# Attention with decay and a switch mixture of experts: from pairs of heads over 512 tokens to 64x64 TensorE tiles over all heads

## Chip, cores and metric

One Trainium2 chip, one core of it. The metric is the device time of one launch in microseconds, and the median of three runs of the kernel before is 514.04 us (512.87 to 514.76). The profile is one execution of its own.

## What is computed

q, k and v have 8 batches, 8 heads, 576 tokens and 64 channels each, in f32. Scores are weighted by a decay per head, without softmax; the 4608 rows of 512 channels then go each to one of 8 experts.

```python
scores = scale * np.matmul(q, k.transpose(0, 1, 3, 2))
gamma = 1.0 - 2.0 ** (-5.0 - np.arange(H, dtype=np.float32))
Dmat = np.where(rel >= 0, gamma[:, None, None] ** rel[None, :, :], 0.0)
ret = scores * Dmat[None, :, :, :]
attn_out = np.matmul(ret, v)
x = attn_out.transpose(0, 2, 1, 3).reshape(B * S, H * D)
logits = x @ w_gate
expert_idx = np.argmax(logits, axis=1)
# gate_w: the chosen expert's softmax probability
out[mask] = gate_w[mask, None] * (np.maximum(xe @ w1[e], 0.0) @ w2[e])
```

## The kernel before

The decay is put into q and k ahead of the products (kg, qg: powers of gamma by position), so a score needs a causal mask alone. What lies further back than the current chunk of 128 tokens comes from a state, the sum of k^T v over the earlier chunks.

**Attention.** The loop runs over units (b, p): for each of 8 batches four units with a pair of heads and 512 tokens in four chunks, and a fifth with the last 64 tokens of all heads. Five functions make a unit. `stage_T` (lines 221 to 258) scales kk and qq on GpSimd, transposes both on TensorE into psq and psk, and copies them to qT (VectorE) and kT (ScalarE). `stage_S` (260 to 274) sums the states of all four chunks with products of 128x64 by up to 256 columns into pss; ScalarE copies them to sall. `stage_SC` (276 to 300) makes scores of 128x128 per head in psa and psb, one head on the upper half of the rows and one on the lower; VectorE multiplies them by the mask tri into sa and sb. `stage_AV` (302 to 326) adds scores times v and state times q in psx, copied to xT. `stage_XR` (330 to 359) turns xT back into rows with a product by iw, the identity with the gate's weights beside it: so rows and logits come at once; ScalarE writes xr in bf16, VectorE adds up lg, and SyncE's queue writes x_rows to DRAM.

TensorE's order is the program's order, fixed by `pin`: SC of a unit, XR of the one ahead, T and S of the next, AV of this one. The other engines' lists are made by a scheduler, and each engine works its list off in order. q, k and v of batch b+1 are asked for at the head of batch b, into two sets of buffers.

**Routing.** The tokens are routed in two halves (g = 0 and 1). `softmax_top1` and `ranks` give each token its expert and its place there; `place` makes one-hot rows rh by place and pay by expert, and a product of them, pspl, gives the list of tokens by slot. Each expert has 256 slots for the first half (ph 0, two blocks) and 384 for all that is left (ph 1, three blocks). The first half is routed amid batches 4 and 5; the second has to wait for the last batch.

**Experts.** `load_w` (line 200) brings a piece of 128x1024 f32 weights into one of four staging buffers and casts it to bf16. A piece of w1 is written in another order of its columns than it is read (line 211). The pieces of experts 0 and 1 come in the attention, one in every second unit, with GpSimd as the named caster; later ones in turn on ScalarE, VectorE and GpSimd (line 594). Three experts' weights have room. Per expert and phase, `gather` fetches rows by an indirect transfer, `trans` transposes them (line 553) into xt, `mm1` (557) multiplies by w1 and takes Relu on ScalarE into ht, `mm2` (573) multiplies by w2, VectorE scales by the gate's weight into ys, and GpSimd issues an indirect transfer to out.

```python
198:    casts = [nc.gpsimd.tensor_copy, nc.scalar.copy, nc.vector.tensor_copy]
211:            casts[eng](out=w1b[:, c, :, :, :].rearrange("p j s m -> p j m s"),
212:                       in_=st[:, :].rearrange("p (j m s) -> p j m s", m=P, s=2))
285:                    mm(ps[:, c, :], kT[r, c * P:(c + 1) * P], qT[r, c * P:(c + 1) * P], True, True)
312:                    mm(psx[j * DH:(j + 1) * DH, c, :], vt[:, c, 2 * p + j, :], d["sc"][j][:, c, :], c == 0, False)
314:                mm(psx[:, c, :], sl[:, p, c - 1, :], qT[:, c * P:(c + 1) * P], False, c == NCH - 1)
```

## Time and profile before

| | |
|---|---|
| median of three runs | 514.04 us |
| the profiled execution | 518.02 us, its span 516.2 us |
| TensorE products, busy | 407.9 us (79%), 3714 records |
| VectorE, ScalarE, GpSimd, busy | 197.2, 186.9, 277.0 us |
| mean granted clock of TensorE | 0.903 of 2.4 GHz |
| moved by DMA | 82.0 MB, 159 GB/s in the mean |

Busy time is an average over stages with different limits, so it is read by stretch. An f32 product has two records on TensorE, a transpose or a bf16 product one. A record's time runs until its result is written; how fast TensorE works is read from the starts of records that follow each other. In a row of a group stands: line, engine, operation, output<-inputs, shapes, count | busy us, mean ns of one | idle us ahead of them and what ended it.

### The profile page before, as it was taken

The numbers are of one execution on the slowest core, as the hardware profiler recorded it, in microseconds if no ns is written. First come the engines' busy times: TensorE is split into PE (matmuls) and PEld (weight loads), VectorE is DVE, ScalarE is ACT, GpSimd is POOL, SyncE is SP. The second block draws the span as 40 slices with busy tenths as digits, with TensorE's granted clock in tenths as the row PEclk, the third lists the DMA queues.
The fourth block names the chain that finished last, engine by engine and source line by source line (L and its number), as shares of the span: only waits on it lengthen the run. The fifth ranks groups of instructions, "written<-read, shape, count | busy, mean of one in ns | idle before, by whom it ended". The sixth has DMA issues, their size and how long they took to land. (4 is left out here: it accounts for less than half of the span.)

```text
span 516.2 us, 9296 instructions
## 1 busy us (share of the span) xinstructions
PE 407.9 (79%) x3714; PEld 303.6 (59%) x3714; DVE 197.2 (38%) x398; ACT 186.9 (36%) x300; POOL 277.0 (54%) x237
## 2 busy tenths in 40 slices
PE   0999999999997999899857777769196590999930
PEld 0888888888876888688735433436044150555610
DVE  4333333333668333533397232554033260233210
ACT  1343334344332344943310163429334160423400
POOL 9433546943475778731034767746646576452320
PEclk9999999999998999899995968869789596899985
DMA  9978989694975979640100326456562653321120
GB/s 207 241 146 205 222 192 255 165 252 134 247 179 127 229 229 279 235 178 1 48 22 28 102 83 253 155 193 249 194 217 89 238 176 139 111 103 74 57 86 12
DMA packets 107509, 81.98 MB, mean 159 GB/s; under 512 B 82879, under 2 KB 95679, under 8 KB 107457
## 3 DMA queue, kind: packets, MB, share of 16 engines
q1 hardware_dynamic: 102336, 66.61, 47.2%
q0 software_dynamic: 5120, 14.69, 8.0%
q8 instruction: 31, 0.51, 0.4%
q14 instruction: 22, 0.17, 0.1%
HBM read 67.13 MB, written 15.20 MB: 159 GB/s over the span
## 5 line engine op out<-in xcount | busy, mean ns | idle before, releaser
L59 PE MATMUL pm<-xt,w1b 128*128 128x256 bf16 (+1 forms) x512 | 79.7, 315 | 31.2 <-ACT ht L570 28.3
L584 POOL DMA_INDIRECT out_dram<-ys,tids x40 | 41.3, 1031 | 113.9 <-DVE ohb L448 29.2
L59 PEld LDWEIGHTS <-w1b 128*128 128x128 bf16 x512 | 52.1, 102 | 57.4 <-issue 35.9
L570 ACT ACTIVATE ht<-pm 128x384 bf16<-128x384 f32 (+1 forms) x96 | 50.0, 535 | 93.3 <-PE pm L59 91.4
L211 POOL CAST w1b<-wst 128x1024 bf16<-128x1024 f32 x16 | 80.0, 5066 | 6.9 <-PE psb L59 2.7
L59 PE MATMUL py<-w2b,ht 128*128 128x512 bf16 x320 | 79.4, 406 | 2.0 <-ACT ht L570 2.0
L231 POOL TENSOR_TENSOR qq<-qt,qg 128x512 f32<-128x512 f32 x32 | 34.8, 1092 | 52.2 <-PE psq L237 37.9
L488 POOL DMA_INDIRECT xg<-x_rows,tidg x40 | 50.3, 1257 | 17.9 <-DVE gat L476 8.4
L289 DVE TENSOR_TENSOR sa<-psa,tri 128x512 f32<-128x512 f32 x32 | 22.4, 700 | 97.8 <-PE psb L59 96.9
L59 PEld LDWEIGHTS <-ht 128*128 128x128 bf16 x320 | 32.4, 104 | 42.2 <-issue 8.0
L59 PE MATMUL psr<-iw,xT 128*128 128x136 f32 (+1 forms) x320 | 48.3, 295 | 4.3 <-ACT xT L316 3.0
L583 DVE TENSOR_SCALAR ys<-py,gat 128x512 f32<-128x512 f32 x40 | 29.8, 753 | 50.4 <-PE py L59 41.9
L59 PE MATMUL psa<-qT,kT 64*128 64x128 f32 (+1 forms) x320 | 43.4, 277 | 3.6 <-DVE qT L242 3.6
L59 PEld LDWEIGHTS psr<-iw,xT 128*128 128x128 f32 (+1 forms) x320 | 39.6, 181 | 9.5 <-ACT xT L316 5.1
L59 PE MATMUL pss<-vt,kk 128*64 128x128 f32 (+3 forms) x512 | 44.0, 317 | 0.0
L59 PE MATMUL psb<-qT,kT 64*128 64x128 f32 (+1 forms) x320 | 43.5, 277 | 0.0
L211 ACT CAST w1b<-wst 128x1024 bf16<-128x1024 f32 x8 | 39.2, 4962 | 8.2 <-DMA wst<-in_moe_w_dram 7.4
L59 PEld LDWEIGHTS psa<-qT,kT 64*128 64x128 f32 (+1 forms) x320 | 36.1, 181 | 8.0 <-issue 3.7
L227 POOL TENSOR_TENSOR kk<-kt,kg 128x512 f32<-128x512 f32 x32 | 33.8, 1056 | 12.8 <-PE pss L59 11.8
L211 DVE CAST w1b<-wst 128x1024 bf16<-128x1024 f32 x8 | 25.9, 3233 | 38.0 <-PE pm L59 25.3
L59 PEld LDWEIGHTS pss<-vt,kk 128*64 128x64 f32 x512 | 33.0, 142 | 12.2 <-issue 6.4
L59 PE MATMUL psx<-qT,sall 128*128 128x128 f32 (+1 forms) x256 | 38.8, 289 | 0.0
(124 smaller groups left out, 615.1 us busy)
## 6 DMA issues: line engine op xcount, KB each, us to landing
wst<-in_moe_w_dram SPq DMA_DIRECT2D x64, 512.0 KB, 4.9
kt<-in_k_dram SPq DMA_DIRECT2D x28, 256.0 KB, 5.5
qt<-in_q_dram SPq DMA_DIRECT2D x7, 1024.0 KB, 7.8
vt<-in_v_dram SPq DMA_DIRECT2D x28, 256.0 KB, 5.1
x_rows<-xr SPq DMA_DIRECT2D x8, 512.0 KB, 3.9
kt<-in_k_dram SPq DMA_DIRECT2D x8, 128.0 KB, 3.8
qt<-in_q_dram SPq DMA_DIRECT2D x4, 256.0 KB, 4.1
vt<-in_v_dram SPq DMA_DIRECT2D x8, 128.0 KB, 3.8
```

The costliest lines, as they stand in the source:

```text
L59: return pin(nc.tensor.matmul(out=out, lhsT=lhsT, rhs=rhs, start=start, stop=stop, skip_group_check=True))
L211: casts[eng](out=w1b[:, c, :, :, :].rearrange("p j s m -> p j m s"), in_=st[:, :].rearrange("p (j m s) -> p j m s", m=P, s=2))
L227: nc.gpsimd.tensor_tensor(out=kk[:, :, :].rearrange("p c (h d) -> p c h d", d=DH), in0=kt[:, :, h0:h0 + 2, :], in1=kg[:, 0:NCH, h0:h0 + 2] ...
L231: nc.gpsimd.tensor_tensor(out=qq[:, :, :].rearrange("p s (h d) -> p h s d", d=DH), in0=qt[:, h0:h0 + 2, :, :], in1=qg[:, 0:NCH, h0:h0 + 2] ...
L289: nc.vector.tensor_tensor(out=sa[:, :, :], in0=psa[:, :, :], in1=m, op=ALU.mult)
L488: nc.gpsimd.indirect_dma_start(out=xg[:, :], out_offset=None, in_=x_rows[0:nr, :], in_offset=bass.IndirectOffsetOnAxis(ap=slots[ph][1][:, ...
L570: nc.scalar.activation(out=ht[:, f0:f0 + per, :], in_=pm[:, :, :], func=AF.Relu)
L583: nc.vector.tensor_scalar(out=ys[:, :], in0=py[:, :], scalar1=gat[:, i:i + 1], scalar2=None, op0=ALU.mult)
L584: nc.gpsimd.indirect_dma_start(out=out[:, :], out_offset=bass.IndirectOffsetOnAxis(ap=tids[:, i:i + 1], axis=0), in_=ys[:, :], in_offset=N ...
```

## The change

The attention goes over blocks (b, c): 128 tokens (c = 0 to 3) of all heads, and the last 64. Scores, the state and the output work in chunks of 64 tokens, all in products of 64x64. S and SC and the first half of AV name four quarters of the array in turn (rows by the half of the operands, columns by the half of the output); the second half of AV, state times q, names the upper left and the lower right one. What the two row halves make goes to two banks: pss and psx have two banks, which VectorE and ScalarE add up (so2, so, se; xo, xT). pss and psx are one tile each for the whole attention. `stage_R` makes rows with transposes, and the gate's logits come once a batch (`stage_L1`, `stage_L2`) with 32 columns of weights per quarter. q of the next batch is transposed in the blocks of this one (`stage_TQ`). TensorE's order per block is S, SC, R of the block ahead, TK of the next, L1, AV, TQ, L2.

w1 and w2 keep their plain layout, so the cast reads and writes straight. The early pieces name ScalarE as caster and come one per block in the last 16 blocks; later ones VectorE, ScalarE, VectorE in turn, GpSimd never. Staging has 3 buffers for 4, gathered rows 6 for 8. `place` is cut in `prep` (all on VectorE), `rows_hot` and the product; the first half's prep for phase 1 moves into the attention.

```diff
-    stpool = ctx.enter_context(tc.tile_pool(name="wstage", bufs=4))
+    stpool = ctx.enter_context(tc.tile_pool(name="wstage", bufs=3))
-    gp = ctx.enter_context(tc.tile_pool(name="gath", bufs=8))
+    gp = ctx.enter_context(tc.tile_pool(name="gath", bufs=6))
...
+    psx = ps1.tile([P, 2, 512], F32, name="psx")
+    nc.vector.memset(psx[:, :, :], 0.0)
+    pss = ps1.tile([P, 2, 512], F32, name="pss")
...
-    casts = [nc.gpsimd.tensor_copy, nc.scalar.copy, nc.vector.tensor_copy]
+    casts = [nc.scalar.copy, nc.vector.tensor_copy, nc.gpsimd.tensor_copy]
...
-            casts[eng](out=w1b[:, c, :, :, :].rearrange("p j s m -> p j m s"),
-                       in_=st[:, :].rearrange("p (j m s) -> p j m s", m=P, s=2))
+            casts[eng](out=w1b[:, c, :], in_=st[:, :])
...
+    def stage_S(b, c):
...
+        for p in range(NP):
+            for par in range(2):
+                r = slice(par * DH, (par + 1) * DH)
+                for j in range(2):
+                    h = 2 * p + j
+                    mm(pss[j * DH:(j + 1) * DH, par, p * DH:(p + 1) * DH], kk[r, h, :], vt[r, c, h, :],
+                       c == 0 and p == 0, c == NCH - 1)
...
+            nc.vector.tensor_tensor(out=fl, in0=e_, in1=sts[(b, c, "oo")][:, :, :].rearrange("p a d -> p (a d)"),
+                                    op=ALU.add)
+        so2 = wkp.tile([P, NP, DH], F32, tag="so2")
+        nc.scalar.copy(out=so2[:, :, :].rearrange("p a d -> p (a d)"), in_=o_)
+        se = wkp.tile([P, NP, DH], F32, tag="se")
+        nc.vector.tensor_tensor(out=se[:, :, :].rearrange("p a d -> p (a d)"), in0=e_,
+                                in1=so2[:, :, :].rearrange("p a d -> p (a d)"), op=ALU.add)
...
+    def stage_SC(b, c):
...
+                    for par in range(2):
+                        t0 = c * P + par * DH
+                        mm(ps[par * DH:(par + 1) * DH, j, p * DH:(p + 1) * DH], kT[r, p, par * DH:(par + 1) * DH],
+                           qT[r, p, t0:t0 + DH], True, True)
...
+        nc.vector.tensor_tensor(
+            out=sc[:, :, 0:n, :], in0=ps[:, :, 0:n * DH].rearrange("p j (a i) -> p j a i", i=DH),
+            in1=tri[:, :].unsqueeze(1).unsqueeze(1).to_broadcast([P, 2, n, DH]), op=ALU.mult)
+
+    def stage_AV(b, c):
...
+                    for j in range(2):
+                        mm(x[j * DH:(j + 1) * DH, par, p, par, :], vt[r, c, 2 * p + j, :], sc[r, j, p, :],
+                           p == 0, False)
+            for p in range(NP):
+                for par in range(2):
+                    for j in range(2):
+                        r = slice(j * DH, (j + 1) * DH)
+                        t0 = c * P + par * DH
+                        mm(x[r, j, p, par, :], (se, so)[par][r, p, :], qT[r, p, t0:t0 + DH], False, p == NP - 1)
...
+        xo = wk1.tile([P, n * P], F32, tag="xo", name="xo")
+        nc.scalar.copy(out=xo[:, :], in_=psx[:, 1, 0:n * P])
...
+        nc.vector.tensor_tensor(out=dst, in0=psx[:, 0, 0:n * P], in1=xo[:, :], op=ALU.add)
...
-        w_at.setdefault(len(units) - 2 * len(early) + 2 * n_, []).append(x_)
+        w_at.setdefault(len(blocks) - len(early) + n_, []).append(x_)
...
+        stage_S(b, c)
+        stage_SC(b, c)
         if i > 0:
-            stage_XR(units[i - 1])
+            stage_R(*blocks[i - 1])
...
+            stage_TK(*blocks[i + 1])
+        if c == 0 and b > 0:
+            stage_L1(b - 1)
+        stage_AV(b, c)
+        if c < NP and b + 1 < B:
+            stage_TQ(b + 1, c)
...
+        if (b, c) == (B // 2 + 2, 0):
+            prep(1, 0, rt)
...
-            load_w(e, pt, (1, 2, 0)[nq[0] % 3])
+            load_w(e, pt, (1, 0, 1)[nq[0] % 3])
...
+            rows_hot(1, 0, rtm2)
+            prep(1, 1, rtm2)
+            rows_hot(1, 1, rtm2)
```

VectorE in the attention, before, one unit with a pair of heads (sa and sb are masked scores, qT the copy of q transposed, lg the logits):

```order
L289 TENSOR_TENSOR sa<-psa,tri 128x512
L290 TENSOR_TENSOR sb<-psb,tri 128x512
L242 COPY qT<-psq 128x512
L350 TENSOR_TENSOR lg<-psr,lg 128x32
L289 TENSOR_TENSOR sa<-psa,tri 128x512
L290 TENSOR_TENSOR sb<-psb,tri 128x512
```

VectorE, the change, two blocks of a batch (in names the list shows so2 as so with a number):

```order
L270 TENSOR_TENSOR so<-pss,so_733 128x256
L275 TENSOR_TENSOR se<-pss,so_864 128x256
L305 TENSOR_TENSOR sc<-pssc,tri 128x512
L354 TENSOR_TENSOR xT<-psx,xo 128x512
L270 TENSOR_TENSOR so<-pss,so_864 128x256
L275 TENSOR_TENSOR se<-pss,so_965 128x256
L305 TENSOR_TENSOR sc<-pssc,tri 128x512
```

The copy of q went to ScalarE, and the sums of the two banks, for the state ahead of the mask and for the output behind it, came to VectorE.

ScalarE, the change, at the start of batch 5 (w2b and w1b are casts of early weights):

```order
L247 COPY kT<-psk 128x512
L346 COPY xo<-psx 128x512
L234 COPY qT<-psq 128x512
L213 CAST w2b<-wst 128x1024 x2
L209 CAST w1b<-wst 128x1024
L273 COPY so_2971<-pss 128x256
L368 CAST xr<-psr 128x512
L247 COPY kT<-psk 128x512
L209 CAST w1b<-wst 128x1024 x2
L346 COPY xo<-psx 128x512
```

Before, these pieces' casts stood in GpSimd's list; here five of them stand among the copies of one block and the next.

GpSimd with the experts, before (xg is a gather, out_dram a scatter):

```order
L584 DMA out_dram<-ys,tids_2041 4608x512 x2
L211 CAST w1b<-wst 128x4x128x2
L488 DMA xg<-x_rows,tidg_3212 128x512 x2
L584 DMA out_dram<-ys,tids_3211 4608x512 x2
L216 CAST w2b<-wst 128x1024
L584 DMA out_dram<-ys,tids_3211 4608x512
```

GpSimd with the experts, the change:

```order
L536 DMA xg<-x_rows,tidg_2946 128x512
L536 DMA xg<-x_rows,tidg_4631 128x512
L643 DMA out_dram<-ys,tids_4630 4608x512 x3
L536 DMA xg<-x_rows,tidg_4631 128x512 x2
L536 DMA xg<-x_rows,tidg_2946 128x512
L643 DMA out_dram<-ys,tids_2945 4608x512 x2
```

The casts are gone from this list; gathers and scatters are left.

## Rows read from the trace of the kernel before

**Rows 1.** Busy time by stretch: us, busy us per engine (x count), PEclk, DMA share, GB/s

```profile
15.90:254.00 238.10, 229.43 (x2651) 198.75 (x2648) 97.61 (x214) 99.13 (x186) 126.71 (x91) 0.99 0.75 189
254.00:280.30 26.30, 15.54 (x115) 10.69 (x116) 23.39 (x84) 3.30 (x6) 8.90 (x4) 0.79 0.10 34
280.30:329.00 48.70, 37.94 (x195) 20.23 (x195) 15.17 (x23) 16.98 (x23) 32.86 (x22) 0.83 0.38 130
329.00:442.80 113.80, 69.36 (x418) 41.09 (x417) 39.09 (x44) 48.73 (x50) 70.67 (x43) 0.79 0.53 190
442.80:495.30 52.50, 51.47 (x321) 29.56 (x318) 14.85 (x26) 16.54 (x32) 21.00 (x21) 0.99 0.21 78
```

**Rows 2.** Timeline of TensorE, one unit with a pair of heads

```profile
107.36 0.37 PE L59 MATMUL psa<-qT,kT 64*128 64x128 f32 x1
...
109.49 0.60 PE L237 MATMUL psq<-ident,qq 128*128 128x128 f32 x4
109.92 0.60 PE L240 MATMUL psk<-ident,kk 128*128 128x128 f32 x4
110.45 1.31 PE L59 MATMUL pss<-vt,kk 128*64 128x256 f32 x16
...
113.43 0.37 PE L59 MATMUL psa<-qT,kT 64*128 64x128 f32 x1
```

**Rows 3.** The same view, 64x64 products of a unit with the last tokens

```profile
99.89 0.22 PE L59 MATMUL psx<-sa,vr 64*64 64x64 f32 x1
99.90 0.22 PE L59 MATMUL psx<-sb,vr 64*64 64x64 f32 x1
99.95 0.22 PE L59 MATMUL psx<-sa,vr 64*64 64x64 f32 x1
...
99.90 0.14 PEld L59 LDWEIGHTS psx<-sb,vr 64*64 64x64 f32 x1
```

**Rows 4.** Groups by line and shape, whole span: copies and sums from PSUM

```profile
L289 DVE TENSOR_TENSOR sa<-psa,tri 128x512 f32<-128x512 f32 x32 | 22.4, 700 | 97.8 <-PE psb L59 96.9 <-PE psa L59 0.9
L298 DVE TENSOR_TENSOR sa<-psa,tri 64x256 f32<-64x256 f32 x8 | 3.3, 414 | 13.5 <-PE psb L59 13.5
L244 ACT COPY kT<-psk 128x512 f32<-128x512 f32 x32 | 18.7, 585 | 18.1 <-PE psk L240 17.5 <-issue 0.6
L257 ACT COPY kT<-psq 128x256 f32<-128x256 f32 x8 | 3.0, 372 | 5.1 <-DVE qT L255 3.3 <-DVE lg L350 1.8
```

**Rows 5.** Who waited for whom: us in total, times, longest us

```profile
DVE lg L350 <- ACT xr L344: 3.7, 2, 2.5
```

**Rows 6.** Groups by line and shape, whole span: casts of weights

```profile
L211 POOL CAST w1b<-wst 128x1024 bf16<-128x1024 f32 x16 | 80.0, 5066 | 6.9 <-PE psb L59 2.7 <-DMA wst<-in_moe_w_dram 2.1 <-PE pm L59 2.1
L211 ACT CAST w1b<-wst 128x1024 bf16<-128x1024 f32 x8 | 39.2, 4962 | 8.2 <-DMA wst<-in_moe_w_dram 7.4 <-PE pm L59 0.8
L216 ACT CAST w2b<-wst 128x1024 bf16<-128x1024 f32 x8 | 8.4, 1045 | 47.7 <-DMA wst<-in_moe_w_dram 42.8 <-PE py L59 4.9
L216 DVE CAST w2b<-wst 128x1024 bf16<-128x1024 f32 x8 | 8.3, 1038 | 34.5 <-DMA wst<-in_moe_w_dram 34.5
```

**Rows 7.** Busy time by stretch, loads of batches 0 and 1 (columns as rows 1)

```profile
4.00:32.00 28.00, 20.29 (x210) 17.31 (x212) 11.38 (x18) 7.24 (x16) 16.87 (x28) 1.00 1.15 235
```

**Rows 8.** Timeline of VectorE, second routing

```profile
270.69 9.49 DVE L461 TENSOR_SCALAR rh<-iota_r,r 128x128 bf16<-128x128 bf16 x38
```

**Rows 9.** The chain that ended last, experts, and a scatter in GpSimd's timeline

```profile
471.60 5.18 PE py L59 x24
476.78 3.49 PE pm L59 x32
...
481.39 3.45 PE py L59 x16
484.85 5.20 PE pm L59 x32
...
500.03 0.97 POOL L584 DMA_INDIRECT out_dram<-ys,tids  x1 [2.53 <-DMA out_dram<-ys,tids]
```

More of the change, by code (lines that the diff above doesn't have):

```diff
@@ L462, in place @@
                                     op0=ALU.is_equal)
[L463 to L464 removed]
+        hot[(ph, g)] = (rh, pay)
+    def place(ph, pool, psp):
+        w = E * ((CA if ph == 0 else CB) // P)
+        for g in range(ph + 1):
+            rh, pay = hot[(ph, g)]
+            for t in range(GT):
+                mm(psp[:, 0:NFLD * w], rh[:, t, :], pay[:, t, :, :].rearrange("p f w -> p (f w)"),
+                   t == 0 and g == 0, t == GT - 1 and g == ph)
@@ L492, in gather @@
             gat_t[(e, ph, j)] = xg
-    units = [(b, p) for b in range(B) for p in range(NP + 1)]
+    blocks = [(b, c) for b in range(B) for c in range(NCOL)]
     rtmp = p1.enter_context(tc.tile_pool(name="rtmp", bufs=1))
```

436 lines of the change are left out of this document (213 added, 223 removed).

## The prediction

> **What bounds the kernel now.** I read the busy time by stretch first [rows 1], to cut the span into stages with different limits. In the attention, 15.9 to 254.0 us, TensorE is busy 229 of 238 us at a granted clock of 0.99, that is at 2.4 GHz. From 254.0 to 280.3 VectorE is busy 23.4 of 26.3 us and TensorE waits for the second routing. From 280.3 to 442.8 the experts run with TensorE busy 107 of 162 us at a clock near 0.8; from 442.8 to 495.3, when all weights are cast, it is busy 51.5 of 52.5 at 0.99. The last 20.9 us of the 516.2 belong to the scatters.
>
> The timeline of TensorE gives the attention's unit: one pair of heads takes 113.43 - 107.36 = 6.07 us [rows 2]. Eight batches take 238.1 us, 29.8 each. The small 64x64 products [rows 3] show what tiles can do: two products to two column tiles start 0.01 us apart, and the next pair follows 0.06 us later. An f32 product has two such records, so a round of two products takes 0.116 us.
>
> Among the groups by line the casts stand out [rows 6]: a piece of w1 takes 5.07 us on GpSimd and 4.96 on ScalarE, a piece of w2, as large but written straight, 1.05 or less. ScalarE and VectorE also stood 42.8 and 34.5 us before w2 casts for weights that came late, since the staging buffers were held by slow casts. Without them the experts' pace would be TensorE's own.
>
> **Attention, TensorE.** Each block of 128 tokens over all heads now has four stages of 16 products of 64x64. Three use four tiles in turn; the state's part of the output uses only the two diagonal tiles, since a head's state and output sit on its own half. No row shows four tiles. Bounds: a round of four lasts as long as a round of two, 0.116 us, or twice that (no gain), or 0.464 us (one after another). I take 0.116: it is the nearest row, and the trace shows pairs by rows (psa and psb) and by columns (sa and sb) overlap alike [rows 2, 3]. Then S, SC and the first half of AV take 4 x 0.116 = 0.46 us each, the second half 8 x 0.116 = 0.93, and three groups of four transposes 0.43 each [rows 2]: 3.6 us. A change of stage costs 0.10 us (psk at 109.92 plus 0.43, pss at 110.45), seven make 0.7: 4.3 us per block.
>
> **Attention, the chain outside TensorE.** The accumulator psx is single, and between two blocks' AV stands: the stream 1.39 us, 0.2 until a reader starts, ScalarE's xo 0.585, VectorE's xT 0.70, so 0.41, ScalarE's so2 0.37, VectorE's se 0.41 and sc 0.70 [rows 4]. so2 comes behind so although both only read pss: two readers of one PSUM tile go one behind the other already now [rows 5]. With six hand-offs of 0.04 and less 0.2 where VectorE's instructions overlap, that is 4.8 us, more than TensorE's 4.3. So a block costs 4.8. The block of the last 64 tokens has no S: its AV is due 4.05 us after the one ahead. From it to the next batch TensorE runs half an AV, S, SC, R, TK and the gate's L1 (about 1 us), 4.4 us with its changes of stage; L2 adds 0.3. A batch is 3 x 4.8 + 4.05 + 4.4 + 0.3 = 23.2 us.
>
> The start is later. All four q pieces are needed ahead of the first block: 2.9 MB at 235 GB/s [rows 7] from 2.3 us on, then transposes, copies, scores and mask: first AV at about 18 us. In block 0 TensorE wants batch 1's q, behind 4.9 MB, at 24 us, and reaches it at 19.5: 4.5 us lost once. Transfers are then hidden: a batch brings 3.54 MB of q, k, v and 0.59 MB of rows, 17.6 us at that rate against 23.2.
>
> The casts of experts 0, 1 and 2 move from GpSimd, where they were off the path, to ScalarE (some to VectorE), into this chain. Work of 1.05 us fits: ScalarE's own sum per block is 2.7 of 4.8 us. The wait doesn't: at the start of batches 4 to 7 the list has two or three casts one block behind their transfers, which stand behind 1.2 MB of v. That is 2.7 MB or 10 us of transfer against 5 us of lead, and everything on ScalarE, kT and xo too, is queued behind. Bounds: 0 (the transfers start earlier than I count) and 50 us (every burst pays all of it twice). I take four bursts of 5 us, 20 us: 5 us is also the mean wait of ScalarE's w2 casts in rows 6, 42.8 us over eight. So the last AV ends at 18 + 4.5 + 7 x 23.2 + 19.5 + 20 = 224 us, against 253.5: **-29.5 us**.
>
> **Routing of the second half.** One-hot rows for half of the tokens are made ahead, 20 of 40 at about 0.25 us [rows 8], but 14 of these stand in VectorE's queue ahead of lt, so 3.5 us come back at once; pay, now on VectorE alone for half of the tokens, costs some 3 us, as much as its share did. Net **-2 us** of the 26.3.
>
> **Experts.** From 280.3 to 329.0 (experts 0 and 1) gathers and a cold clock stay; a cast of 5 us that held ScalarE and a wait for w2 go: **-9 us**. From 329.0 to 495.3, six experts take 166 us. At TensorE's pace two blocks and three blocks take 3.49 + 3.45 + 5.20 + 5.18 us [rows 9] and 1.8 for five blocks of transposes and their copies, 19.1 in all. GpSimd now only gathers and scatters: five scatters at 3.5 us apiece (0.97 and a wait of 2.53 for the one ahead [rows 9]), with gathers partly between, 19 us, so it is no gain to run faster. I take 19.5, 117 us: **-49 us**. Fewer staging buffers (3 for 4) cost nothing while TensorE has four units of lead on each weight; without that lead each fourth piece would cost a transfer, about 3 us per unit. The tail of 20.9 us stays.
>
> Sum: -29.5 - 2 - 9 - 49 = -89.5. The profiled execution took 518.0 us (span 516.2), so 428.5; the three runs' median, 514.0, lies 0.8% below it, which makes **425 us**.
>
> A rule that speaks against this: the Trainium skill, "TensorE: Matmul & The Clock Gate", Part 3 (Packing small matmuls), says that a weight load overlaps a running product only where the row group differs. By that rule the two column tiles of one row group would wait for each other's loads. The trace disagrees: sb's load of 0.14 us begins at 99.90 amid sa's product, on the same rows, and the pairs keep their 0.06 us [rows 3].
>
> **Rivals.** (a) Four tiles give no more than two. For: loads double per round. Against: instructions are issued within 0.01 us [rows 3]. Stages become 0.93, TensorE bound: 0.93 x 4 + 1.29 + 0.7 = 5.7 us per block, near 29 per batch; the ScalarE waits partly hide, the attention loses 10 us against before: about 465 us. (b) The casts wait more on ScalarE, 50 us instead of 20, since with four pieces of weights a batch wants 6.2 MB, 26 us at the rate of rows 7, against 23.2: 455. (c) The experts don't reach TensorE's pace, because weights (37 pieces of 0.52 MB in 117 us), scatters and gathers (2.0 MB per expert) want some 270 GB/s, more than the 235 of rows 7: 24 us per expert as a price between 19.5 and today's 28: 452. (d) The four tiles run one after another: a round of four takes 0.464, a block 3 x 1.86 + 0.93 x 2 + 1.29 + 0.7 = 9.4 us, a batch some 45: 8 x 15 = 122 us more than now, less 60 for the rest: slower, about 575. This decides from a round of about 0.36 us on (a batch of 37 us); pairs that overlap speak against it. (e) A chain a little shorter or longer leaves the time within 0.5% only if gains and losses cancel; I see no mechanism. That the change doesn't do what it says is excluded by the lists: GpSimd has no cast left.
>
> **Numbers.** My forecast 0.62, with its own range 400 to 448 (cast waits 0 to 40, 18.9 to 21 us per expert); (a) 0.12, (b) 0.13, (c) 0.09, (d) 0.03, (e) 0.01. The range 394 to 468 takes in (a), (b) and (c) at their prices. A measurement of this kernel tells some 0.5% from no change: faster 0.96, same 0.01, slower 0.03.
>
> **What would show it.** Right: records of all four tiles within 0.06 us; blocks of 4.8 us with TensorE waiting for sc behind VectorE; ScalarE waiting for weight transfers some 20 us in the attention; its end near 225 us; w1 casts of 1.05 us; experts every 19 to 20 us at a clock near 1; the same tail. Wrong: rounds of four above 0.15 us, blocks above 5.5 us without waits for casts, a granted clock that falls in the attention, or scatters that wait for each other while TensorE stands.

## The result: 467 us where 425 were forecast

The changed kernel takes 466.96 us (median of four runs, 462.46 to 471.44) against 513.54 for the kernel before on the same chip: 0.906 of it, 95% interval 0.899 to 0.913. The forecast was 425 with a range of 394 to 468. The sign is right and the time lies within the range, one us below its upper end, but outside the forecast's own 400 to 448; the gain is 47 us where 89 were worked out. The range reached this far because it took in the rivals' prices, and none of the rivals came true by its own mechanism (below): that the time fell into it is luck.

The profiled execution took 471.44 us with a span of 469.6. It is the longest of the four, at a mean granted clock of 0.909 where the other three show 0.920 to 0.930; f0, below, repeats its stages in an execution of 469.04 us. The sum of the prediction, made against the span of before, ends at 516.2 - 89.5 = 426.7, so 42.9 us are to be found. Busy time by stretch of the changed kernel (columns as [rows 1]):

```profile
21.00:244.20 223.20, 176.12 (x5122) 152.94 (x5121) 99.44 (x236) 106.81 (x195) 72.22 (x69) 0.94 0.73 196
244.20:270.40 26.20, 20.22 (x189) 13.59 (x189) 19.59 (x85) 4.26 (x8) 2.44 (x2) 0.77 0.08 27
270.40:307.00 36.60, 33.37 (x204) 19.66 (x204) 13.51 (x28) 12.94 (x23) 17.43 (x17) 0.93 0.61 205
307.00:406.00 99.00, 80.42 (x487) 46.24 (x485) 35.66 (x61) 33.97 (x58) 40.77 (x40) 0.90 0.63 217
406.00:443.00 37.00, 36.41 (x240) 22.07 (x239) 10.45 (x18) 12.62 (x24) 14.09 (x15) 1.00 0.24 85
```

The attention's last product AV ends at 245.5 us, 21 us later than the 224 forecast; from there to the last product of the second routing are 25.1 us, where the kernel before took 27.1 (253.5 to 280.5), so the 2 us of the forecast came; experts 0 and 1 take 36 us (forecast 40); experts 2 to 7 end at 444.1, 23.0 us each where 19.5 were forecast, which is 21 us. The tail is 469.6 - 444.1 = 25.5 us, 4.6 more than before. Together (21 - 4 + 21 + 5) these differences make up the 43 us. TensorE is no longer the bound of the attention: it is busy 176 of 223 us, and its granted clock fell from 0.99 to 0.94. In the last stretch, when all weights are cast, an expert takes 18 to 19 us, as forecast.

One block of 128 tokens, in the timeline of TensorE, ScalarE and VectorE near the end, where little is transferred:

```profile
230.95 0.69 PE L59 MATMUL psx<-sc,vt 64*64 64x64 f32 x32 [0.72 <-ACT kT L247]
...
232.26 0.27 PE L59 MATMUL pss<-vt,kk 64*64 64x64 f32 x2
...
232.67 0.58 ACT L346 COPY xo<-psx 128x512 f32<-128x512 f32 x1 [1.77 <-PE psx L59]
232.77 0.22 PE L59 MATMUL pssc<-qT,kT 64*64 64x64 f32 x1
...
233.29 0.69 DVE L354 TENSOR_TENSOR xT<-psx,xo 128x512 f32<-128x512 f32 x1 [2.48 <-ACT xo L346]
233.89 0.41 DVE L270 TENSOR_TENSOR so<-pss,so 128x256 f32<-128x256 f32 x1
...
235.08 0.68 DVE L305 TENSOR_TENSOR sc<-pssc,tri 128x512 f32<-128x512 f32 x1
...
235.91 0.69 PE L59 MATMUL psx<-sc,vt 64*64 64x64 f32 x32 [0.79 <-ACT kT L247]
```

From one first half of AV to the next are 4.96 us (4.8 forecast), and 16 products on four tiles take about 0.5 us: the first of S starts at 232.26, the first of SC at 232.77 (0.46 forecast). Between the two AV stands the chain of the forecast: xo, xT, so, then ScalarE's so2 (234.34) and VectorE's se (234.74), and sc. The last row names ScalarE's kT as what TensorE waited for, but its products read sc, which ends at 235.76, 0.04 us ahead of kT. But few blocks look like this one. The starts of the masked scores, VectorE's row that leads into AV, give the batches (counted from 1 here, so the routing that the program puts amid b = 4 and 5 falls into batches 5 and 6); here the first rows of batches 4 to 8, and below them TensorE's last AV products:

```profile
96.36 0.69 DVE L305 TENSOR_TENSOR sc<-pssc,tri 128x512 f32<-128x512 f32 x1 [0.73 <-PE pssc L59]
...
125.53 0.68 DVE L305 TENSOR_TENSOR sc<-pssc,tri 128x512 f32<-128x512 f32 x1
...
159.18 0.67 DVE L305 TENSOR_TENSOR sc<-pssc,tri 128x512 f32<-128x512 f32 x1
...
189.76 0.68 DVE L305 TENSOR_TENSOR sc<-pssc,tri 128x512 f32<-128x512 f32 x1
...
223.72 0.68 DVE L305 TENSOR_TENSOR sc<-pssc,tri 128x512 f32<-128x512 f32 x1
...
244.89 0.65 PE L59 MATMUL psx<-kT,se 64*64 64x64 f32 x16
```

Batches 4 to 7 take 29.2, 33.7, 30.6 and 34.0 us against the 23.2 of the forecast (plus 5 each for waits of casts). The casts themselves are as short as forecast, but they wait; groups by line and shape, whole span:

```profile
L209 ACT CAST w1b<-wst 128x1024 bf16<-128x1024 f32 x16 | 16.7, 1046 | 15.9 <-DMA wst<-in_moe_w_dram 15.7 <-PE pm L59 0.2
L213 ACT CAST w2b<-wst 128x1024 bf16<-128x1024 f32 x16 | 16.7, 1048 | 38.6 <-DMA wst<-in_moe_w_dram 38.6
```

A piece of w1 takes 1.05 us, where it took 4.96 and 5.07 [rows 6]. The waits in these two rows, 54 us, are those of the whole span; 17.4 of them lie between 121 and 250 us, in the attention.

In the experts, who waited for whom from 307 to 406 us, and one such wait in the timeline:

```profile
DVE ys L642 <- DMA out_dram<-ys,tids: 23.7, 8, 6.4
...
PE pt L612 <- DVE xt L613: 15.4, 4, 4.9
```

```profile
336.65 0.75 DVE L642 TENSOR_SCALAR ys<-py,gat 128x512 f32<-128x512 f32 x1 [3.49 <-DMA out_dram<-ys,tids]
337.32 1.28 DVE L213 CAST w2b<-wst 128x1024 bf16<-128x1024 f32 x2
...
338.52 0.74 DVE L613 COPY xt<-pt 128x512 bf16<-128x512 bf16 x2
338.98 0.59 PE L612 MATMUL pt<-identb,xg 128*128 128x128 bf16 x4 [4.92 <-DVE xt L613]
```

VectorE waits with ys until a scatter four blocks back has landed, since ys has four buffers; behind ys stand two casts, and behind these the copy xt that frees TensorE's next transposes: TensorE stands 4.92 us. The scatters go one behind the other to the end; GpSimd's timeline:

```profile
453.59 0.98 POOL L643 DMA_INDIRECT out_dram<-ys,tids  x1 [2.51 <-DMA out_dram<-ys,tids]
457.09 0.98 POOL L643 DMA_INDIRECT out_dram<-ys,tids  x1 [2.52 <-DMA out_dram<-ys,tids]
```

TensorE is done at 444.1; four scatters are issued after that, 3.5 to 3.8 us apart, the last two of which stand here. From the start of its issue to its landing a scatter takes 2.6 us at the least and 2.9 in the median of 40. That agrees with the Trainium skill, "DMA: Bandwidth & Descriptors", section Anatomy of one DMA, which gives a transfer issued by GpSimd some 2 us plus its bytes, about 2.6 us for these 256 KB as an estimate by its formula. The step of the chain, 3.5 us from one scatter to the next, is longer than the landing itself.

### The profile page after: what moved, and what is told of

It is laid out like the page before. It is cut to its first block, busy times and chain, and to the rows that moved or that the text cites. A ratio compares the mean times of both kernels' runs of the same rounds, so it can differ in the third digit from the quotient of the medians.

```text
span 469.6 us, 14468 instructions
## 1 busy us (share of the span) xinstructions
PE 355.6 (76%) x6322; PEld 260.7 (56%) x6322; DVE 183.8 (39%) x436; ACT 175.5 (37%) x316; POOL 164.0 (35%) x198
## 5 line engine op out<-in xcount | busy, mean ns | idle before, releaser
L225 POOL TENSOR_TENSOR qq<-qt,qg 128x512 f32<-128x512 f32 x32 | 33.8, 1060 | 90.5 <-PE psq L231 67.2
L59 PEld LDWEIGHTS <-ht 128*128 128x128 bf16 x320 | 32.3, 103 | 39.0 <-issue 8.6
L354 DVE TENSOR_TENSOR xT<-psx,xo 128x512 f32<-128x512 f32 x32 | 22.0, 689 | 61.8 <-ACT xo L346 61.7
L346 ACT COPY xo<-psx 128x512 f32<-128x512 f32 (+1 forms) x40 | 21.7, 544 | 56.3 <-PE psx L59 56.3
L59 PE MATMUL psx<-sc,vt 64*64 64x64 f32 x1024 | 23.6, 234 | 18.1 <-DVE sc L305 15.7
L59 PE MATMUL psx<-qT,so 64*64 64x64 f32 x512 | 33.5, 223 | 0.5 <-issue 0.5
L231 PE MATMUL psq<-ident,qq 128*128 128x128 f32 x128 | 23.3, 309 | 13.6 <-POOL qq L225 12.4
L59 PEld LDWEIGHTS psx<-sc,vt 64*64 64x64 f32 x1024 | 19.2, 143 | 24.9 <-DVE sc L305 20.9
L366 PE MATMUL psr<-ident,xT 128*128 128x128 f32 x128 | 22.2, 299 | 14.2 <-DVE xT L354 14.1
L213 ACT CAST w2b<-wst 128x1024 bf16<-128x1024 f32 x16 | 16.7, 1048 | 38.6 <-DMA wst<-in_moe_w_dram 38.6
L612 PE MATMUL pt<-identb,xg 128*128 128x128 bf16 x160 | 14.4, 230 | 20.6 <-DVE xt L613 17.4
L368 ACT CAST xr<-psr 128x512 bf16<-128x512 f32 (+1 forms) x40 | 23.3, 584 | 16.8 <-PE psr L366 16.7
L59 PEld LDWEIGHTS psx<-qT,so 64*64 64x64 f32 x512 | 28.5, 139 | 0.0
L59 PE MATMUL pssc<-qT,kT 64*64 64x64 f32 x1024 | 24.2, 230 | 5.4 <-issue 3.6
```

What stands on the lines that cost most here:

```text
L59: return pin(nc.tensor.matmul(out=out, lhsT=lhsT, rhs=rhs, start=start, stop=stop, skip_group_check=True))
L225: nc.gpsimd.tensor_tensor(out=qq[:, :, :].rearrange("p s (h d) -> p h s d", d=DH), in0=qt[:, h0:h0 + 2, :, :], in1=qg[:, 0:NCH, h0:h0 + 2] ...
L231: pin(nc.tensor.transpose(out=pst[:, s_:512:NCH], in_=qq[:, s_, :], identity=ident[:, :]))
L346: nc.scalar.copy(out=xo[:, :], in_=psx[:, 1, 0:n * P])
L354: nc.vector.tensor_tensor(out=dst, in0=psx[:, 0, 0:n * P], in1=xo[:, :], op=ALU.add)
L366: pin(nc.tensor.transpose(out=ps[0:n, p * P:(p + 1) * P], in_=src, identity=ident[:, :]))
```

## The experiments

All but the first measurement ran on four other chips (e1 to e4 on one, f0 to f3, g1 to g3 and h1 on one each), where the kernel before takes 520 to 523 us, so ratios to it are compared. Stages come from one profiled execution each: start of the last masked scores, end of the second routing (the last product pspl), TensorE's last product, span (us). No ratio stands on record for e1, so its median and spread are given.

| run | ratio to before (95%) | last sc | routing | TensorE | span |
|---|---|---|---|---|---|
| changed, first chip | 0.906 (0.899 to 0.913) | 242.8 | 270.6 | 444.1 | 469.6 |
| f0 changed again | 0.899 (0.894 to 0.905) | 240.4 | 267.3 | 441.6 | 467.2 |
| e1 five staging buffers | 469.3 us (461.9 to 473.9) | 238.8 | 266.6 | 443.1 | 465.5 |
| e2 eight ys buffers | 0.903 (0.898 to 0.907) | 238.5 | 263.7 | 434.6 | 463.0 |
| e3 scatters to four tensors | 0.861 (0.857 to 0.866) | 237.9 | 261.9 | 430.1 | 444.4 |
| f1 all three | 0.830 (0.826 to 0.834) | 234.4 | 261.6 | 419.3 | 433.4 |
| e4 early casts on GpSimd | 0.891 (0.886 to 0.897) | 242.3 | 270.3 | 441.7 | 467.6 |
| f2 no weights in the attention | 0.893 (0.889 to 0.897) | 221.3 | 256.8 | 438.4 | 462.9 |
| g1 before, plain weights alone | 0.923 (0.917 to 0.929) | | 271.7 | 452.7 | 478.9 |
| g2 two tiles in turn | 0.913 (0.907 to 0.920) | 246.2 | 272.5 | 445.8 | 472.9 |
| g3 weights late | 0.878 (0.871 to 0.886) | 227.9 | 257.2 | 428.0 | 457.1 |
| h1 routing spread, gathers ahead | 0.872 (0.867 to 0.878) | 228.7 | 262.2 | 425.4 | 465.0 |

**f0, the changed kernel again.** No edit.

> The changed kernel unedited, to have it beside the other runs on the same chip and to see how far its stages spread from one execution to the next: 462 to 472 us on a chip like the first, TensorE's experts about 173 us, the tail 25 us, batches 4 to 7 within 2 us of 29, 34, 31 and 34.

469.77 us (468.20 to 471.53), 0.899 of before. Batches 4 to 7 take 28.1, 33.8, 31.5 and 33.1 us, TensorE's experts 441.6 - 267.3 = 174.3, the tail 25.6. These stages repeat within 2 us, and differences below that are not read. The attention as a whole spreads more: from batch 1's first masked scores to batch 8's it takes 202.7 us in the first chip's profile, 201.0 here, and 199.3 and 198.6 in e2 and e3, whose edits don't touch it.

### The experts

**e1, five staging buffers.**

```diff
-    stpool = ctx.enter_context(tc.tile_pool(name="wstage", bufs=3))
+    stpool = ctx.enter_context(tc.tile_pool(name="wstage", bufs=5))
```

> One edit: five staging buffers for weights instead of three. In the changed kernel (466.96 us) TensorE with the experts takes 18 to 19 us per expert once all weights are cast (406 to 443 us), but 23 to 27 us from 307 to 406 us. Theory A, the casts' buffers: a transfer waits until one of three buffers is cast, and the casts stand behind other work in VectorE's and ScalarE's lists; with five buffers the waits of w2 casts for transfers (38.6 us on ScalarE, 17.6 on VectorE) fall by half and more, and the time falls by 8 to 20 us, the upper end only if the scatters (3.5 us apiece, 40 of them) can follow. Theory B, the chain of scatters holds VectorE and thereby the casts: within 4 us of the changed kernel. Theory C, transfers are at their rate: within 4 us, with the same waits of ScalarE.

469.26 us, not to be told from f0. ScalarE's wait of w2 casts for transfers fell from 27.9 to 4.7 us, and TensorE's experts took no less time, 176.5 us (waits of this kernel from 262 to 445 us):

```profile
PE pt L612 <- DVE xt L613: 17.5, 6, 6.2
...
ACT w2b L213 <- DMA wst<-in_moe_w_dram: 4.7, 2, 3.9
```

TensorE waits for xt as long as in the changed kernel (17.4). Theory A alone falls: three staging buffers are no loss against five while the rest stays, as forecast for three against four.

**e2, eight ys buffers.**

```diff
-    yp = p2.enter_context(tc.tile_pool(name="yp", bufs=4))
+    yp = p2.enter_context(tc.tile_pool(name="yp", bufs=8))
```

> One edit: eight buffers for the scaled rows ys instead of four, so VectorE waits for a landed scatter only eight blocks back; the lists of all engines stay as they are. VectorE's wait of ys for scatters (35.8 us) goes to nearly 0 in every theory. Theory B, this wait holds the casts and transposes behind it: 10 to 20 us less than 466.96. Theories A and C, the weights are late for other reasons and the wait only fills time: within 3 us.

470.54 us. TensorE's experts take 170.9 us, 3 less, and the tail is 3 longer. The wait for xt fell, and another stands in its place (2.2 us in the changed kernel):

```profile
PE pt L612 <- DMA xg<-x_rows,tidg: 11.2, 5, 6.4
```

The wait for xt is 4.9 us now. The gathers come late, which stand behind waiting scatters in GpSimd's list. Theory B alone, in the form that ys holds the casts, falls too.

**e3, scatters to four tensors.**

```diff
+    outs = [out] + [dram.tile([NTOK, DM], F32, name=f"alt{a}") for a in range(3)]
...
-                out=out[:, :], out_offset=bass.IndirectOffsetOnAxis(ap=tids[:, i:i + 1], axis=0),
+                out=outs[(j + 2 * ph + e) % 4][:, :], out_offset=bass.IndirectOffsetOnAxis(ap=tids[:, i:i + 1], axis=0),
```

> Left out of the output: scatters go in turn to out and to three scratch tensors, so three quarters of the rows are missing from out. No scatter waits for the one ahead; each then takes GpSimd about 1.3 us instead of 3.5. The last five scatters, which today start 0 to 14 us after TensorE's last product (442.9 to 457.1 us), start within 6 us of it: 8 to 12 us less in every theory. Theory B, the chain also sets the experts' pace from 307 to 406 us: 20 to 30 us less in all. Theory A or C, weights set it: 8 to 13 us less.

448.62 us, 0.861: 20 us less than f0 by the ratios. 11 us of it are the tail (14.3 us), 6 TensorE's experts (168.2); the last scatter starts at 431.17, 1 us behind TensorE. What is left lies ahead of the experts (the routing ends 5 us earlier than in f0), where the edit changes nothing. The chain of scatters sets the end, but alone not the pace.

**f1, the three edits together.**

> The edits of e1, e2 and e3 in one (five staging buffers, eight ys buffers, scatters in turn to four tensors; three quarters of the rows missing from out). Alone they left TensorE's experts (end of the second routing to its last product) at 176.5, 170.9 and 168.2 us against 173.5. Theory D, three covers of about the same length, each of which shows when another is taken away (scatters that hold ys and with it VectorE's copies xt; casts on VectorE that wait for weights ahead of xt; gathers behind scatters): together 145 to 158 us, and the total 435 to 445. Theory C, transfers of weights are at their rate while all weights are brought (0.89 of the time busy at 296 GB/s from 300 to 345 us in e3): 164 to 170 us, no more than e3.

434.14 us, 0.830. TensorE's experts take 157.7 us. Busy time by stretch of this kernel (columns as rows 1):

```profile
300.00:400.00 100.00, 94.43 (x618) 57.00 (x626) 41.12 (x70) 40.16 (x70) 50.21 (x48) 1.00 0.65 233
```

From 300 us on TensorE is busy 94 of 100 us at full clock, and the transfers keep up at 233 GB/s in the mean: theory C, that their rate is the limit, falls. Theory D holds (145 to 158 us, and 435 to 445 in all). Against 174.3 us the edits alone gave +2, -3 and -6, together -17: covers hid each other. No two of the edits were run without the third, so whether all three are needed is not shown.

### The attention

**e4, early casts on GpSimd.**

```diff
-            load_w(e, pt, 0)
+            load_w(e, pt, 2)
```

> One edit: the 16 casts of experts 0 and 1 name GpSimd, as before the change, in the plain layout. Theory of the prediction: their waits for transfers on ScalarE (17.4 us between 121 and 250 us) hold kT and xo, so batches 4 to 7, which take 29 to 34 us instead of 23.5, lose 3 us less each: 8 to 15 us less than 466.96. Rival R1: GpSimd's kk and qq wait in their place, and the pace stays: within 4 us. Rival R2: the first routing on VectorE and TensorE's own stalls make these batches long: within 4 us, with ScalarE's waits gone. A straight cast on GpSimd has no row; between 1.05 us (a product of the same size there) and 5.07 us (the strided cast).

468.52 us, 0.891. Batches 4 to 7 take 25.3, 34.0, 32.0 and 34.2 us: 125.6 in all, f0 126.5. The casts take 1.04 us there. Batch 4 is 3 us shorter, as the theory has it, the others are not. In batch 7 the casts of expert 2, which stay where they were, wait 9.9 us for transfers on ScalarE and 9.9 on VectorE, the longest 5.8 and 7.0 (in f0 all casts of weights there wait 8.5 and 5.0). So the caster named for the early pieces does not decide the pace; as waits of other casts grew in their place, this run does not clear ScalarE's and VectorE's lists.

**f2, no weights in the attention.** The staging buffers are taken only behind the attention.

```diff
-    early = [(e, i) for e in range(2) for i in range(8)]
+    early = []
...
     p1.close()
+    stpool = ctx.enter_context(tc.tile_pool(name="wstage", bufs=3))
```

> Weights are staged only once the attention is over, so ScalarE and VectorE have no cast in it and no weight transfer runs beside it; the experts then start late and the total says nothing. Read from its attention: theory of the prediction, waits of casts cost about 20 us: batches 4 to 7 (first masked scores of a batch to those of the next) fall from 29, 34, 31, 34 to 24 to 26 each, the last masked scores come at 215 to 222 us instead of 238 to 243. Rival R2, routing on VectorE and TensorE's own stalls: batch 5 stays above 30 us, and the others above 26.

The first masked scores of batches 4 to 8:

```profile
94.93 0.68 DVE L305 TENSOR_TENSOR sc<-pssc,tri 128x512 f32<-128x512 f32 x1
...
118.17 0.68 DVE L305 TENSOR_TENSOR sc<-pssc,tri 128x512 f32<-128x512 f32 x1
...
149.82 0.67 DVE L305 TENSOR_TENSOR sc<-pssc,tri 128x512 f32<-128x512 f32 x1
...
179.73 0.68 DVE L305 TENSOR_TENSOR sc<-pssc,tri 128x512 f32<-128x512 f32 x1
...
203.14 0.68 DVE L305 TENSOR_TENSOR sc<-pssc,tri 128x512 f32<-128x512 f32 x1
```

Batches 4 and 7 fall to 23.2 and 23.4 us; batches 5 and 6 stay at 31.6 and 29.9. Theory and rival both hold, each for its batches. From batch 1's first row to batch 8's this kernel needs 203.1 - 21.2 = 181.9 us, f0 on the same chip 222.0 - 21.0 = 201.0: weights in the attention cost **19 us** (17 to 21 with the spread of f0's repeats); the prediction had 20. They are not the four equal bursts of the prediction: batches 4 to 7 lose 4.9, 2.1, 1.6 and 9.7 us by them. This edit takes away the casts and their transfers at once, so what of the 19 us is waits of casts and what the transfers cost the loads beside them is not shown. The total is unexpected: with all weights late it is no longer than f0's. The stretch from the last masked scores to the routing's end grew from 26.9 to 35.4 us and TensorE's experts from 174.3 to 181.6, so the early weights give back there only what they take from the attention.

**f3, no loads either.** Batches 3 to 8 use q, k and v of the first two, so the output repeats two batches. Its time of 6057 us is that of the program's last part, for tokens beyond an expert's slots; only the attention is read.

```diff
     def load_batch(b, first):
+        if b > 1:
+            return loads[b - 2]
```

> As f2, and from the third batch on q, k and v are those of the first two (the output is wrong: six batches repeat two). After batch 1's loads no transfer but that of x rows runs beside the attention. Theory: TensorE's pauses that wait for nothing the profile shows (1.5 us at 50, 61 and 95 us, about 8 us in all up to 121 us) come from its instructions arriving late behind the loads: they vanish, blocks take 4.9 to 5.0 us as in batch 8, batches 23.4 us or less except where the routing is (batches 5 and 6). Rival: they belong to TensorE's program, and batches 2 to 4 stay at 25 to 27 us.

```profile
90.10 0.68 DVE L305 TENSOR_TENSOR sc<-pssc,tri 128x512 f32<-128x512 f32 x1
...
113.29 0.68 DVE L305 TENSOR_TENSOR sc<-pssc,tri 128x512 f32<-128x512 f32 x1
...
145.59 0.67 DVE L305 TENSOR_TENSOR sc<-pssc,tri 128x512 f32<-128x512 f32 x1
...
175.85 0.68 DVE L305 TENSOR_TENSOR sc<-pssc,tri 128x512 f32<-128x512 f32 x1
...
199.04 0.68 DVE L305 TENSOR_TENSOR sc<-pssc,tri 128x512 f32<-128x512 f32 x1
```

Batches 4 and 7 take 23.2 us, the forecast to the tenth; 5 and 6 take 32.3 and 30.3. So the first routing costs 32.3 + 30.3 - 2 x 23.2 = **16.2 us**, with no transfer of q, k, v or weights about, and loads cost f2's 181.9 less 178.2 here = **3.7 us**. With these three the attention adds up: 7 batches at 23.2 are 162.4 us, f0 takes 38.6 more, and 19.1 + 16.2 + 3.7 are 39.0. In the loads' share stand pauses of TensorE that the trace puts down to nothing. One of the changed kernel's (others are 1.33 us at 50.66 and 1.54 at 61.62), and below it the only one of over 0.4 us in f3 up to 230 us, at the time of batch 2's load:

```profile
95.94 0.38 PE L59 MATMUL pssc<-qT,kT 64*64 64x64 f32 x9 [1.57 <-issue]
```

```profile
26.11 0.49 PE L366 MATMUL psr<-ident,xT 128*128 128x128 f32 x3 [0.82 <-issue]
```

That they come with the loads is shown; that TensorE's instructions arrive late behind them is argued: the page's queue for instructions moved 0.84 MB against 0.51 before.

### Parts of the change

**g1, the kernel before with plain weights alone.**

```diff
-            casts[eng](out=w1b[:, c, :, :, :].rearrange("p j s m -> p j m s"),
-                       in_=st[:, :].rearrange("p (j m s) -> p j m s", m=P, s=2))
+            casts[eng](out=w1b[:, c, :],
+                       in_=st[:, :])
...
-            load_w(e, pt, (1, 2, 0)[nq[0] % 3])
+            load_w(e, pt, (2, 1, 2)[nq[0] % 3])
```

> The kernel before with the experts' part of the change alone: plain layout of w1 and w2, later casts on VectorE, ScalarE, VectorE in turn, early casts still on GpSimd, four staging buffers as before. Theory: the part of the change behind the attention stands by itself; from the end of the second routing to TensorE's last product the changed kernel takes 173 to 174 us where the kernel before takes 215, and its tail is 5 us longer: 32 to 40 us less than before, 0.925 to 0.94 of it, and the attention as before. Rival: without the shorter attention the weights come earlier against the experts and more is won: 45 us and over. Rival: the strided casts were hidden, as GpSimd and ScalarE had time: under 12 us less.

The edit lays out w2's rows plainly too (not shown). 480.49 us, 0.923: 40 us less than before. So most of the change's gain comes without a new attention: by the ratios, 0.024 or 12 us (8 to 17 by their intervals) are left for all the rest of the change. Part of the 40 us stands in the attention itself. The first of the last tokens' products of batches 5 and 7, in the kernel before and then here:

```profile
158.05 0.27 PE L59 MATMUL psx<-sa,vr 64*64 64x64 f32 x1
...
225.32 0.27 PE L59 MATMUL psx<-sa,vr 64*64 64x64 f32 x1
```

```profile
157.95 0.27 PE L59 MATMUL psx<-sa,vr 64*64 64x64 f32 x1
...
216.52 0.27 PE L59 MATMUL psx<-sa,vr 64*64 64x64 f32 x1
```

Two batches, 6 and 7, lie between these rows: 67.3 us before, 58.6 here, where other two took 58.5 before (99.55 to 158.05). So the casts as they were (strided, and some of the later ones on other engines) had held the old attention back by 9 us, though in the kernel before TensorE was the engine that bound it. The trace of the kernel before shows how:

```profile
156.14 7.00 DVE L461 TENSOR_SCALAR rh<-iota_r,r 128x128 bf16<-128x128 bf16 x5
157.62 4.72 POOL L211 CAST w1b<-wst 128x1024 bf16<-128x1024 f32 x1
...
163.34 0.34 PE L59 MATMUL psa<-qT,kT 64*128 64x128 f32 x1 [3.57 <-DVE qT L242]
```

Five one-hot rows took VectorE 7.00 us, where seven had taken 1.22 just before. The last of the five began at 157.65, 0.03 us behind GpSimd's strided cast, and ended at 163.14, 5.50 us later, with GpSimd's next instruction (kk, to 163.09). qT stood behind it, and TensorE waited 3.57 us for qT. In this run the cast takes GpSimd 1.03 us, the row that begins beside it 1.05, and TensorE doesn't wait. Two more strided casts stood on ScalarE at 204.1 and 210.0 us, 4.76 us each, and TensorE waited 2.56 us for ScalarE's xT at 210.14. These are TensorE's only waits of over 0.2 us in the two batches, 6.1 us of the 9; the other 3 are busy time, 60.9 us for 58.0, at a granted clock of 0.95 for 1.00 (0.66 in the 5 us behind the first wait).

With casts of 1.04 us the last AV product of the old attention ends at 244.7 us, that of the new one at 245.5, and at 243.1, 241.3 and 240.6 in f0, e2 and e3: **beside the same weights the new attention gains 0 to 4 us**, hardly more than its spread. An undisturbed batch does gain, 23.2 us (batch 4 of f2) for 28.5 (99.88 less 71.35 here), but waits for weights and routing eat it up. Most of the 12 us lies behind the attention: against f0's 243.1 its end accounts for 1.6, f0's routing takes another 3 less, and TensorE's experts take 452.7 - 271.7 = 181 us here for f0's 174.3 (the tail 26.2 for 25.6). Which of the change's other edits brings that was not run.

**g2, two tiles in turn.** The same products, ordered by row half in S, SC and the first half of AV; AV's loops:

```diff
-            for p in range(NP):
-                for par in range(2):
+            for par in range(2):
+                for p in range(NP):
                     r = slice(par * DH, (par + 1) * DH)
                     for j in range(2):
```

> Same products, same tiles, another order: S, SC and the first half of AV run all products of one row half ahead of those of the other, so neighbours in the order share a row half and only two of the four tiles take turns. Theory: 16 products then take 0.93 us, as the second half of AV does on its two tiles, where four in turn take 0.51; of the three stages only AV lies on the chain of a block (S and SC run while ScalarE and VectorE make xo and xT), so a block is 0.4 to 0.5 us longer, 32 blocks and 8 batch changes 14 to 24 us: 1.03 to 1.05 of the changed kernel run beside it on such a chip (469.8). Rival (a) of the prediction, four in turn give no more than two: within 3 us, and stages of equal length.

474.45 us, 0.913 against 0.899 for f0, some 7 us. The first half of AV in one block and the next:

```profile
233.54 0.80 PE L59 MATMUL psx<-sc,vt 64*64 64x64 f32 x26 [0.46 <-DVE sc L305]
...
238.79 0.80 PE L59 MATMUL psx<-sc,vt 64*64 64x64 f32 x26 [0.79 <-ACT kT L247]
```

A clean block takes 5.25 us instead of 4.96, since its 16 products need 0.82 us (228.28 to the second half's 229.10, a block before) instead of 0.5. Rival (a) falls: four in turn are faster than two. The worth is smaller than I wrote (14 to 24 us), because 0.93 was too long for these two tiles: 0.3 us in 32 blocks are 10. That the rest of it hides in blocks that wait for something else is argued.

### A version after these readings

**g3, weights late.** Expert 0's weights go into the buffers of q, k and v that batch 7 leaves empty, cast on GpSimd; all else is staged behind the attention in six buffers.

```diff
+        if (b, c) in ((B - 1, 0), (B - 1, 2)):
+            for g_, p0 in ((("q", 0), ("k", 2), ("v", 4)) if c == 0 else (("k", 6),)):
+                kv = ldp.tile([P, 4 * F // 2], F32, tag=g_, name="kv")
+                for a in range(2):
+                    load_w(0, p0 + a, 2, kv[:, a * F:(a + 1) * F])
...
+    stpool = p2.enter_context(tc.tile_pool(name="wstage", bufs=6))
...
-    yp = p2.enter_context(tc.tile_pool(name="yp", bufs=4))
+    yp = p2.enter_context(tc.tile_pool(name="yp", bufs=8))
```

> A version that should beat both: only expert 0's weights come in the attention, in batch 7 into buffers of q, k and v that nobody fills any more, cast on GpSimd; expert 1's on GpSimd during the second routing; all later ones into six staging buffers that take the attention's memory; eight ys buffers; two of five pay products of the first half on GpSimd. Theory: batches 2 to 5 and 8 go at 23.2 to 26 us as in f2, the two with the routing at 29 to 32, last masked scores at 216 to 222 us; second routing 25 to 28 us; TensorE's experts 155 to 168, since the ys and the staging covers go but scatters still follow each other 3.5 us apart; tail 25 to 29 us: 438 to 455 in all, 0.84 to 0.87 of before. Rival: transfers of 24 pieces of weights at once with the experts' start hold TensorE there as in f2 (181.6 us): 455 to 468.

457.22 us (454.63 to 460.37), 0.878: faster than the changed kernel, but above the 438 to 455 expected and within the rival's 455 to 468, though not for the rival's reason, which had 181.6 us for the experts. What failed is the attention, which ends 12 us earlier than f0's, not 20: batches 4 to 7 take 23.2, 34.2, 28.3 and 25.8 us. TensorE's experts take 170.8 us (expected 155 to 168); its longest wait there is 8.2 us for a gather, and the tail is 29.1 us.

**h1, routing spread.** g3 with VectorE's order in the attention written out, a piece of routing behind each block's masked scores, and gathers issued three units ahead.

```diff
         stage_SC(b, c)
+        step(b, c)
...
-        if i + 2 < len(seq):
-            gather(*seq[i + 2])
+        for n_ in ((2, 3) if i == 0 else (i + 3,)):
+            if n_ < len(seq):
+                gather(*seq[n_])
```

> g3 with two edits. First, VectorE's order in the attention is written out: the first half's routing comes in pieces of 0.9 to 2.9 us, one per block, behind the masked scores, where VectorE waits 2.4 us for xo, and all of it stays on VectorE. Theory E, the two batches with the routing (32.3 and 30.3 us without any load in f3, 34.2 and 28.3 in g3, against 23.2) are long because routing work stands in VectorE's list ahead of so, se, sc and xT: they fall to 24 to 27 us each, and the last masked scores come at 214 to 221 us instead of 228. Rival: the routing's products, its waits on TensorE or the clock make them long: 29 us and more each. Second, gathers are issued three units ahead instead of two, with eleven buffers: TensorE's wait for gathers (16.6 us in g3, one of 8.2) falls below 6 us. In all 440 to 450 us, 0.845 to 0.865 of before; since the scatters, 3.5 us apart, are the last to end, TensorE's gain behind 330 us only makes the tail longer.

457.81 us (451.31 to 466.77), 0.872 (0.867 to 0.878): not to be told from g3, and above the 440 to 450 expected. The stages below are those of its longest execution (466.77 us). First masked scores of batches 5 to 8:

```profile
123.56 0.69 DVE L223 TENSOR_TENSOR sc<-pssc,tri 128x512 f32<-128x512 f32 x1 [0.37 <-PE pssc L59]
...
148.64 0.68 DVE L223 TENSOR_TENSOR sc<-pssc,tri 128x512 f32<-128x512 f32 x1
...
175.57 0.68 DVE L223 TENSOR_TENSOR sc<-pssc,tri 128x512 f32<-128x512 f32 x1
...
207.00 0.68 DVE L223 TENSOR_TENSOR sc<-pssc,tri 128x512 f32<-128x512 f32 x1
```

Batches 5 and 6 fall to 25.1 and 26.9 us from 34.2 and 28.3, as theory E has it. But batch 7, where the pieces for phase 1 went, rose from 25.8 to 31.4: the three together take 83.4 us against 88.2. The pieces are not all of that rise. In the batch's longest block, 8.8 us from one masked scores to the next, the products of S, which take 0.5 us elsewhere, run from 187.69 to 191.08 with four pauses of 0.2 to 0.4 us that wait for nothing the profile shows, and VectorE, done with its piece, stands idle:

```profile
187.69 0.84 PE L59 MATMUL pss<-vt,kk 64*64 64x64 f32 x17
...
191.01 0.69 DVE L223 TENSOR_TENSOR xT<-psx,xo 128x512 f32<-128x512 f32 x1 [3.56 <-issue]
```

Four gathers and transfers of weights run beside it, at 238 GB/s, and the granted clock is 0.78 there. So how much of the routing's price was removed and how much moved is open. Batch 2, which has neither routing nor weights, took 30.7 in this execution, with pauses of 1.6 and 2.9 us in TensorE's products. TensorE's wait for gathers fell to 5.0 us and its last product came at 425.4, but the last scatter left at 452.1: the chain of scatters takes what the rest gains.

## Why the prediction was half right

**The two TensorE steps held.** Four tiles are used at once (16 products in 0.5 us, forecast 0.46), and a block is a chain through ScalarE and VectorE of 4.96 us (forecast 4.8). Without other work a batch takes 23.2 us, as summed, though here errors cancel: in batch 4 of f3 the first three intervals take 15.45 us for 14.4, the last two 7.74 for 8.75. Rivals (a) and (d) fall. The rule quoted in the prediction (the Trainium skill, "TensorE: Matmul & The Clock Gate", Part 3) gives a weight load no overlap with running products of its own row group. [rows 3] show a load that does overlap so, but the times leave open what the rule is worth here: in the four-tile order two of each four neighbours share a row group and 16 products take 0.5 us; g2, where all but one pair of neighbours share one, is slower, 0.82, as the rule would have it; but the two diagonal tiles, which never share one, need 0.93.

**The waits of early casts: right in size, 19 us for 20, and partly by luck.** The loss is not spread as the prediction had it (9.7 us in batch 7, 1.6 in batch 6, for 5 in each), and that it comes by ScalarE's list is not shown: e4 moved 16 casts and the pace stayed, while the casts left on ScalarE and VectorE waited longer. The lead was misworked on the way: 2.7 MB at 235 GB/s are 11.5 us and not 10, which the 5 us per burst did not use.

**The step that failed in the attention** is the one that was not in the sum: the first half's routing. I priced the second routing alone ("pay, now on VectorE alone for half of the tokens, costs some 3 us"). In the kernel before TensorE was the bound and VectorE's routing lay beside it (g1's batch with the routing takes 29.5 us, those ahead of it 28.5); the change made VectorE part of the block's chain, so some 22 us of VectorE's work in these two batches became 16.2 us of time. I had summed ScalarE's work per block ("2.7 of 4.8 us") and never VectorE's with the routing in it. The loads' share, 3.7 us, was not seen either. My start was right only in sum: first AV at 21.7 us for 18, but no wait of 4.5 for batch 2's q.

**A step right in the sum for a wrong reason.** The early casts move "from GpSimd, where they were off the path": the strided casts were not, they held the old attention back by 9 us (g1). Since I summed the new attention from zero, the error touched no number, but it hid that plain casts alone would bring g1's 40 us, and that the 29.5 us booked for the new attention (8 came, from 253.5 to 245.5) would then be no gain of the tiles.

**The experts.** "I take 19.5" was mis-sized: 23.0, close to the 24 of rival (c), but not for its reason, since f1 has the same transfers and reaches 157.7 us. I judged each engine by its own work (TensorE 19.1, scatters 19) and added nothing for what in-order lists of nearly equal load do to each other: a late scatter stops ys, ys the casts and xt, xt TensorE, and a waiting scatter the gathers. That "it is no gain to run faster" named the scatters as the next bound, which f1 shows; that they hold TensorE up as well I had not seen. It shows in the tail too, which I left at 20.9 and which measured 25.5. "Fewer staging buffers (3 for 4) cost nothing" held as far as e1 shows it, five against three.

**What the indicators said.** A clock that falls in the attention (0.94), blocks above 5.5 us without waits for casts (6.9 us from 119.87 to 126.76 in f3, in the routing) and scatters that wait while TensorE stands were named as what would make the prediction wrong. All three came.

## What to carry to other kernels

When an engine stops being the bound, go through every list that lay beside it: work that was nearly free (here routing on VectorE) stands in the new chain at most of its price, 16 of some 22 us. Price a stage not by its busiest engine but by what its in-order lists do to each other, and when two covers of like length are suspected, remove them together: here three edits gave 2, -3 and -6 us alone and -17 at once. And run the small part of a change by itself: plain casts on the kernel before brought 40 of the 47 to 53 us and left the new attention 0 to 4.

## What the runs showed of the hardware that I had not expected

- TensorE pauses of 0.4 to 1.8 us (2.9 in h1) that wait for nothing the profile shows, in a stream of 64x64 products, beside loads: without loads (f3 behind 30 us) none is over 0.4.
- A one-hot row takes VectorE 0.25 us, but 5.50 us where it began beside a GpSimd cast of 4.72 us, and 1.05 beside one of 1.03 (under g1): both times it ended within 0.05 us of GpSimd's work.
- A wait costs more than itself: behind the 4.92 us at 338.98 the 16 products py that follow took from 339.36 to the next stage at 344.83, 5.47 us, where 16 others took from 312.75 to 316.20, 3.45; the granted clock of TensorE from 339.36 to 344.83 was 0.63 in the mean, so most of that stretch went at the lower level (1.2 GHz).
- Executions of the changed kernel spread from 462.5 to 471.4 us (1.9%), those of the kernel before beside them from 512.9 to 514.8 (0.4%); f0's spread from 468.2 to 471.5 (0.7%).
